# A weight load at the start of a TensorE-bound kernel is made to wait for a one-column activation

## The chip, the cores and the metric

The kernel runs on one core of one Trainium2 chip. The metric is device time in microseconds (us) of one execution. "Span" is the time from the first to the last instruction of a profiled execution; it is about 1.7 us shorter than the time of the same execution. The spread of executions is given as lowest to highest.

## The reference, cut to what matters

```
qkv = x @ wqkv                                  # x: 2048 x 1024, bf16
A:  pq, pk = phi(q), phi(k);  phi(t) = where(t > 0, t + 1, exp(t)) + 1e-6
    a = linear attention of pq, pk, v, 32 heads of 32, then @ wo
B:  sliding window of 8 keys, dilation 2, softmax, then @ wo   (own weights, same x)
out = g * a + (1 - g) * b,   g = sigmoid(sum(x * gate_w))
```

The kernel first computes K of branch A, which is x @ (1024 columns of wqkv), and for that it needs x transposed and these weights.

## The kernel before

The weights of K lie in two tiles, `WkA[0]` and `WkA[1]`: one for the first 512 columns ("first half"), one for the last 512 ("second half"). Each tile is loaded in four quarters of two 128-row blocks of the weights, 256 KB each. `xT` is x transposed by DMA. These are the loads at the start, in program order; SyncE (`nc.sync`) and ScalarE (`nc.scalar`) each issue on a DMA queue of their own:

```python
    nc.scalar.preload_act_table_set("natural_log_exp_and_others")
    ...
    def load_xT(k, t0, t1):
        nc.sync.dma_start_transpose(out=xT[:, 2 * k:2 * k + 2, t0 * P:t1 * P],
                                    in_=rows(x, t0 * P, t1 * P)[:, 2 * k * P:(2 * k + 2) * P])

    def load_wk(eng, k, h):
        eng.dma_start(out=WkA[h][:, 2 * k:2 * k + 2, :],
                      in_=A_wqkv[2 * k * P:(2 * k + 2) * P, D + 512 * h:D + 512 * h + 512]
                      .rearrange("(kt p) n -> p kt n", p=P))

    ones = nc.const_aps.tensor(1.0, [P, P], BF16)
    with tc.manual_schedule(engines={SP, mybir.EngineType.Activation}):
        load_wk(nc.scalar, 0, 0)                       # first half, first quarter
        first_act = consts.tile([P, 1], BF16, name="first_act")
        nc.scalar.activation(out=first_act[:], in_=ones[:, 0:1], func=ACT.Exp)
        load_wk(nc.scalar, 0, 1)                       # second half, first quarter
        load_xT(0, 0, 2)                               # first transpose
        load_xT(0, 2, 4)                               # second transpose
        for k in range(1, 4):
            load_wk(nc.sync, k, 0)
            load_xT(k, 0, 4)
            load_wk(nc.sync, k, 1)
        ...
```

TensorE runs 37 small warm-up matmuls and then the real ones. The order of its first sixteen is fixed: four with the first transpose and the first half, four with the second transpose and the first half, then eight with the second half.

```python
            warm_up(37)
            ...
            for k in range(4):
                for half in range(2):
                    for t in range(4):
                        for kt in (2 * k, 2 * k + 1):
                            project(first[4 * half + t], t, kt, half)
            ...
```

The softmax here doesn't subtract the row's maximum and nothing guards it: scores larger than these inputs give would overflow.

## Time and profile before

| | before |
|---|---|
| time, median of 3 (lowest to highest) | 474.03 us (473.62 to 474.06) |
| span of the profiled execution | 472.3 us |
| TensorE busy | 466.0 us |
| first real matmul | 5.56 us |

Two lines of the page: the busy time and share of each engine, and the chain of work that ended last, by engine.

```profile
PE 466.0 (99%) x5734; PEld 244.7 (52%) x5765; DVE 277.4 (59%) x601; ACT 169.1 (36%) x273; POOL 15.4 (3%) x30
...
PE 98%; DMA 1%; issue 0%; ACT 0%
```

TensorE is the limit nearly everywhere; the only other part of the chain is 1% of DMA. The chain in order of time says where that is (start, duration, what):

```profile
0.80 4.71 DMA xT<-in_A_x_dram
5.51 0.04 issue
5.56 3.16 PE pk_ps L169 x12
```

The first transpose holds the chain until it lands at 5.51 us. The timeline (start, duration, engine, line, operation, what it writes and reads; in brackets the idle time before it and what ended it), first for ScalarE and its DMA queue (ACTq), then for TensorE:

```profile
0.80 1.28 ACT L68 ACT_TABLE_LOAD   x1 [0.80 <-PEq L628]
0.83 0.96 ACTq L98 DMA_DIRECT2D WkA<-in_A_wqkv_dram  x2
2.09 0.20 ACT L106 ACTIVATE first_act<-const-bfloat16-1.0 128x1 bf16<-128x1 bf16 x1
...
0.84 4.11 PE L175 MATMUL warm<-const-bfloat16-1.0 128*128 128x128 bf16 x37 [0.84 <-PEq L628]
5.56 3.81 PE L169 MATMUL pk_ps<-WkA,xT 128*128 128x512 bf16 x14 [0.61 <-DMA xT<-in_A_x_dram]
```

Both weight quarters are issued one right after the other (x2, from 0.83 us) although an activation stands between them in the program: ScalarE's sequencer passes the activation on to the engine, which is busy with its table load, and goes on to the next DMA. TensorE then idles for 0.61 us.

Two stretches of the table by windows (start:end, length, busy time of PE, PEld, DVE, ACT and POOL, clock record, DMA share, GB/s):

```profile
3.50:4.00 0.50, 0.50 (x8) 0.50 (x6) 0.00 (x0) 0.00 (x0) 0.00 (x0) 1.00 1.14 288
4.00:4.50 0.50, 0.50 (x7) 0.50 (x6) 0.00 (x0) 0.00 (x0) 0.00 (x0) 1.00 1.08 331
```

The DMA engines are full here (shares of 1.14 and 1.08: by this measure no idle time is left). The clock column shows 1.00 also where the trace has no clock record yet, as here, so it does not show that the clock was full. By the trace's packets it is mostly the second weight quarter that moves in these two stretches.

### The profile page before, as it was taken

What the parts mean: (1) busy time and instruction counts of PE and PEld (TensorE: products, weight loads), DVE (VectorE), ACT (ScalarE), POOL (GpSimd) and SP (SyncE); (2) the same over time, 40 slices, a digit from 0 to 9 for tenths busy, and PEclk for the clock granted to TensorE, in tenths of its full rate; (3) what the DMA queues carried; (4) which work ended last, traced back from release to release, by engine and by line L of the source; (5) the groups of instructions that cost most, each with busy time, mean ns of one, the idle gap of its engine ahead of it and who ended that gap; (6) DMA issues with size and microseconds to landing.
All of it is one profiled execution on the core that took longest, in us unless ns stands there. A gap on an engine that the chain in (4) does not pass through costs nothing.

```text
span 472.3 us, 13144 instructions
## 1 busy us (share of the span) xinstructions
PE 466.0 (99%) x5734; PEld 244.7 (52%) x5765; DVE 277.4 (59%) x601; ACT 169.1 (36%) x273; POOL 15.4 (3%) x30
## 2 busy tenths in 40 slices
PE   8999999999999999999999999999999999999997
PEld 5444444445444444445666666666664444444444
DVE  0496689990329999999567676767560049800000
ACT  1343321102443333333555555555551134221122
POOL 3300000500000000000000000000000000000000
PEclk9999999999999999999999999999999999999999
DMA  8999970000634233527326526452563933211001
GB/s 212 212 242 374 348 239 0 0 1 0 203 123 125 95 141 129 156 96 247 107 54 108 105 53 95 100 95 51 92 158 79 196 97 78 71 53 46 34 33 46
DMA packets 98780, 55.40 MB, mean 117 GB/s; under 512 B 70178, under 2 KB 90658, under 8 KB 98722
## 3 DMA queue, kind: packets, MB, share of 16 engines
q1 hardware_dynamic: 93282, 49.84, 41.1%
q10 hardware_dynamic: 5440, 4.72, 3.0%
q8 instruction: 45, 0.74, 0.7%
q14 instruction: 13, 0.11, 0.1%
HBM read 26.10 MB, written 15.86 MB: 89 GB/s over the span
## 4 chain that ended last, share of the span: by engine, by line
PE 98%; DMA 1%; issue 0%; ACT 0%
PE q_ps L388 27%; PE d_ps L585 12%; PE pk_ps L169 12%; PE p_ps L295 12%; PE g_ps L220 12%; PE e_ps L585 11%; PE p_ps L331 9%; PE po L467 2%; PE s2b L445 2%; DMA xT<-in_A_x_dram 1%; PE kv_ps L240 0%; PE w_ps L283 0%; ACT osb L590 0%
## 5 line engine op out<-in xcount | busy, mean ns | idle before, releaser
L388 PE MATMUL q_ps<-xT,WqB 64*64 64x512 bf16 x1024 | 68.3, 377 | 0.0
L388 PE MATMUL q_ps<-xT,WkB 64*64 64x512 bf16 x1024 | 67.9, 377 | 0.0
L156 DVE TENSOR_SCALAR e<-e 128x512 f32<-128x512 f32 x64 | 27.0, 423 | 64.3 <-ACT e L155 64.3
L295 PE MATMUL p_ps<-WvB,xT 128*128 128x512 bf16 x250 | 57.3, 379 | 0.5 <-issue 0.3
L169 PE MATMUL pk_ps<-WkA,xT 128*128 128x512 bf16 x251 | 55.6, 381 | 0.9 <-DMA xT<-in_A_x_dram 0.6
L220 PE MATMUL g_ps<-pk,xrow 128*128 128x512 bf16 x251 | 55.2, 379 | 0.3
L450 ACT ACTIVATE PT<-s2b 128x928 bf16<-128x928 f32 (+4 forms) x40 | 34.2, 854 | 45.5 <-PE s2b L445 45.5
L452 DVE TENSOR_TENSOR PT<-PT,mask 128x928 bf16<-128x928 bf16 (+4 forms) x40 | 23.6, 590 | 38.2 <-ACT PT L450 38.2
L331 PE MATMUL p_ps<-WqA,xT 128*128 128x512 bf16 x187 | 43.1, 379 | 0.3
L585 PEld LDWEIGHTS <-pqT 128*128 128x128 bf16 x272 | 26.0, 98 | 29.8 <-issue 0.4
L585 PEld LDWEIGHTS <-OBT 128*128 128x128 bf16 x272 | 26.0, 98 | 29.3
L169 PEld LDWEIGHTS <-xT 128*128 128x128 bf16 x256 | 25.1, 98 | 31.2 <-DMA xT<-in_A_x_dram 0.9
L220 PEld LDWEIGHTS <-xrow 128*128 128x128 bf16 x256 | 25.0, 98 | 30.2
L295 PEld LDWEIGHTS <-xT 128*128 128x128 bf16 x256 | 24.6, 98 | 30.0 <-issue 0.9
L388 PEld LDWEIGHTS <-WkB 64*64 64x64 bf16 x1024 | 31.7, 107 | 15.4 <-issue 0.4
L388 PEld LDWEIGHTS <-WqB 64*64 64x64 bf16 x1024 | 31.4, 106 | 15.4 <-issue 0.7
L155 ACT ACTIVATE e<-pk_ps 128x512 f32<-128x512 f32 x32 | 18.9, 597 | 40.8 <-PE pk_ps L169 36.6
L300 ACT CAST tmp<-p_ps 128x512 bf16<-128x512 f32 x32 | 18.8, 590 | 37.9 <-PE p_ps L295 29.2
L585 PE MATMUL d_ps<-WoA,pqT 128*128 128x512 bf16 (+1 forms) x133 | 30.7, 369 | 0.2
L585 PE MATMUL d_ps<-WoB,OBT 128*128 128x512 bf16 (+1 forms) x134 | 30.7, 369 | 0.1
L331 PEld LDWEIGHTS <-xT 128*128 128x128 bf16 x192 | 18.8, 98 | 22.7
L585 PE MATMUL e_ps<-WoB,OBT 128*128 128x512 bf16 (+2 forms) x133 | 29.7, 363 | 0.2
(62 smaller groups left out, 484.6 us busy)
## 6 DMA issues: line engine op xcount, KB each, us to landing
vd<-tmp SPq DMA_DIRECT2D x16, 264.0 KB
xrow<-in_A_x_dram SPq DMA_DIRECT2D x4, 1024.0 KB
out_dram<-osb ACTq DMA_DIRECT2D x31, 128.0 KB
pqd<-tmp SPq DMA_DIRECT2D x12, 256.0 KB
WvA<-in_A_wqkv_dram SPq DMA_DIRECT2D x2, 1024.0 KB
WoA<-in_A_wo_dram SPq DMA_DIRECT2D x2, 1024.0 KB
WvB<-in_B_wqkv_dram SPq DMA_DIRECT2D x2, 1024.0 KB
WqA<-in_A_wqkv_dram SPq DMA_DIRECT2D x2, 1024.0 KB
```

Of the source, the lines that this page charges most:

```text
L155: nc.scalar.activation(out=e[:], in_=pj[:], func=ACT.Exp)
L156: nc.vector.tensor_scalar(out=e[:], in0=e[:], scalar1=1.0, scalar2=1e-6, op0=ALU.min, op1=ALU.add)
L169: nc.tensor.matmul(pj[:], lhsT=xT[:, kt, t * P:(t + 1) * P], rhs=WkA[half][:, kt, :], start=(kt == 0), stop=(kt == KT - 1))
L220: nc.tensor.matmul(pj[:], lhsT=xrow[:, t, kt * P:(kt + 1) * P], rhs=pk[:, t, half * 512:(half + 1) * 512], start=(t == 0), stop=(t == NB - 1))
L295: nc.tensor.matmul(st["pj"][:], lhsT=xT[:, kt, t * P:(t + 1) * P], rhs=WvB[half][:, kt, :], start=(kt == 0), stop=(kt == KT - 1))
L300: nc.scalar.copy(out=v[:, half * 16:(half + 1) * 16, 0:Dh], in_=st["pj"][:].rearrange("p (h e) -> p h e", h=16))
L331: nc.tensor.matmul(st["pj"][:], lhsT=xT[:, kt, t * P:(t + 1) * P], rhs=WqA[half][:, kt, :], start=(kt == 0), stop=(kt == KT - 1))
L388: nc.tensor.matmul(banks[o][64 * j:64 * j + 64, :], lhsT=lhsT(r, kt, j), rhs=rhs(r, kt), start=first and kt == 0, stop=kt == KT - 1, skip_ ...
L445: nc.tensor.matmul(s2b[64 * par:64 * par + 64, pair, :, o:o + w], lhsT=kts[c][r, par, k0:k0 + 64], rhs=qz[r, :, par, q0 % 512:q0 % 512 + w ...
L450: nc.scalar.activation(out=pt[:, :, 0:W_], in_=s2b[:].rearrange("p a b s -> p (a b) s")[:, :, 0:W_], func=ACT.Exp, scale=SCALE)
L452: nc.vector.tensor_tensor(out=pt[:, :, 0:W_], in0=pt[:, :, 0:W_], in1=mask[:, None, base:base + W_].broadcast_to([P, 4, W_]), op=ALU.mult)
L585: nc.tensor.matmul(st["ps"][:, 0:n], lhsT=lhsT, rhs=W[c0 // 512][:, c, c0 % 512:c0 % 512 + n], start=(side == 0 and c == 0), stop=(side == ...
```

## The change

The activation now writes a column of the second half's tile. The load of that quarter overwrites the column, so it has to wait for the activation. The result is the same. The intent: keep the quarter off the DMA engines while the first transpose, on which TensorE waits, is under way. The whole diff:

```diff
         load_wk(nc.scalar, 0, 0)
-        first_act = consts.tile([P, 1], BF16, name="first_act")
-        nc.scalar.activation(out=first_act[:], in_=ones[:, 0:1], func=ACT.Exp)
+        nc.scalar.activation(out=WkA[1][:, 0, 0:1], in_=ones[:, 0:1], func=ACT.Exp)
         load_wk(nc.scalar, 0, 1)
         load_xT(0, 0, 2)
         load_xT(0, 2, 4)
```

## The prediction

> **What bounds the kernel now.** TensorE. The page gives PE 466.0 of 472.3 us (99%); the chain that ended last is 98% PE, 1% DMA. The list of waits has three for PE: 0.8 us at launch, 0.61 us for the first DMA of xT, 0.3 us of issue. So a moved load can help only at the start. The timeline shows 37 warm-up matmuls from 0.84 to 4.95 us, then idle until the first real matmul at 5.56.
>
> **What the change does.** The 0.205 us activation now writes a column of the second half's weight tile, so the DMA that fills that quarter (256 KB, queued from ScalarE) must wait for it. Before, ScalarE's sequencer issued both weight quarters at 0.83 and 1.35 us (0.446 us each), while the 1.28 us table load and the activation (2.09 to 2.29) still ran; the order staggered nothing. The Trainium skill ("DMA: Bandwidth & Descriptors", Anatomy of one DMA) says that DMA engines don't wait on semaphores; the wait sits on the issuing sequencer. So I expect the second issue at about 2.3 to 2.4 us: about 1.0 us later.
>
> **What it is worth.** Packets of the trace: the first quarter moves from 1.75 to 3.3 us, the first xT transpose from 2.75 to 3.9, the second quarter from 3.5 to 4.5, though issued 1.7 us earlier: it queues behind the first quarter. The first transpose's last data packets end near 3.9, yet its closing 4-byte packets run from 4.25 on and it lands at 5.51. A later transpose has its closing packets right behind the data. So about 0.4 us of the first landing looks like contention with the second quarter (same skill page, Queues, rings and completion order: each engine alternates between queues at packet granularity). The delayed issue could give back at most the 0.61 us wait. But an issue at 2.35 to 2.8, plus the 0.5 us from end of issue to first packet seen for the first quarter, starts its packets at about 3.3 anyway, nearly where they start now. So I expect part: first real matmul at about 5.25 us, 0.3 us earlier, range 0 to 0.6.
>
> **What could be lost.** The second quarter lands now at 5.19 us; delayed by up to 1 us, at most about 6.2. PE needs it after eight matmuls (about 2.3 us in the present timeline), at 7.5 us or later. The second transpose (now 5.91) is needed four matmuls after the first; 6.3 would still just do. Later loads keep about 1 us of slack. Nothing after the start changes.
>
> **Prediction.** 474.03 - 0.3 = 473.7 us, 80% range 473.0 to 474.5. Faster by over 2%: 0.01; within 2%: 0.98; slower by over 2%: 0.01. A 2% move would need 9.5 us; the stretch touched is 5 us.
>
> **What the profile would show.** Right: the second weight issue on ScalarE's queue at about 2.3 us, after the activation; PE's wait on "DMA xT" below 0.61 us (0.1 to 0.5), first real matmul at 5.0 to 5.5 us; no new PE wait on WkA; PE busy still near 466. Wrong: the first xT landing unchanged (then contention was not its cause); a PE wait on WkA between 6 and 9 us.
>
> **What would make it wrong.** The second transpose, not the second quarter, may be what holds back the first one's completion: then nothing moves. The postponed packets may delay the second transpose and create a wait after four matmuls. Removing the one-column tile can shift later tiles' addresses, whose effect I can't cost.

## The result, and the profile after

| | before | after |
|---|---|---|
| time, median of 6 (lowest to highest) | 473.86 us (473.54 to 475.84) | 475.36 us (474.67 to 476.80) |
| ratio | | 1.0029, 95% interval 1.0006 to 1.0052 |
| span of the profiled execution | 472.3 us | 473.0 us |

A ratio is the mean time of one kernel's fast runs over that of the other's in the same rounds, so it is not quite the ratio of the medians. The change is within 2%, but it costs about 1.5 us in the median where 0.3 us of gain was expected. The range of 473.0 to 474.5 us was missed.

The same views of the kernel after: the chain in order of time, then the timeline of ScalarE and of TensorE.

```profile
2.16 5.23 DMA xT<-in_A_x_dram
7.39 0.05 issue
7.44 4.71 PE pk_ps L168 x21
```

```profile
0.82 0.45 ACTq L98 DMA_DIRECT2D WkA<-in_A_wqkv_dram  x1
2.09 0.21 ACT L105 ACTIVATE WkA<-const-bfloat16-1.0 128x1 bf16<-128x1 bf16 x1
2.32 0.41 ACTq L98 DMA_DIRECT2D WkA<-in_A_wqkv_dram  x1
...
0.84 4.11 PE L174 MATMUL warm<-const-bfloat16-1.0 128*128 128x128 bf16 x37 [0.84 <-PEq L627]
5.29 1.04 PE L168 MATMUL pk_ps<-WkA,xT 128*128 128x512 bf16 x4 [0.35 <-DMA xT<-in_A_x_dram]
7.44 1.90 PE L168 MATMUL pk_ps<-WkA,xT 128*128 128x512 bf16 x8 [1.11 <-DMA xT<-in_A_x_dram]
```

The second quarter is issued at 2.32 us, right after the activation ends at 2.30: the intended wait is there. The first real matmul starts at 5.29 us, 0.26 us earlier. But after four matmuls TensorE stands still until 7.44 us, and the chain names the load it waits for: issued at 2.16 us, it is the second transpose, and it lands at 7.39 us. Before, it had landed at 5.91 us and nobody waited for it.

The table by windows, same stretches:

```profile
3.50:4.00 0.50, 0.50 (x8) 0.50 (x7) 0.00 (x0) 0.00 (x0) 0.00 (x0) 1.00 0.28 61
4.00:4.50 0.50, 0.50 (x7) 0.50 (x6) 0.00 (x0) 0.00 (x0) 0.00 (x0) 1.00 0.51 95
```

Where 288 and 331 GB/s had flowed, 61 and 95 flow now. By the packets, the quarter moved from 3.4 to 4.6 us before; after, it trickles from 3.9 to 6.5 us, together with the second transpose (3.6 to 6.0 us).

How much of the time is decided in these first microseconds? Let the "fifth matmul" be the first real one that needs the second transpose. It starts at 6.83 us before and 7.44 after, 0.605 us later, and the spans differ by 0.7 us. The 0.605 us split into three parts, read from the starts of the single matmuls:

- the first matmul starts 0.263 us earlier (gain);
- the first two take 0.442 us instead of 0.829, because in the trace before they ran at half speed: the clock record of that trace begins at full speed at 6.41 us, that of the trace after at 4.83 us (0.387 us; nothing shows that this comes from the change: in e1 below, the same kernel as after, the record begins at 5.66 us);
- the third and fourth, with the wait, take 1.701 us instead of 0.446 (loss of 1.255 us).

### The profile page after: what moved, and what is told of

Its sections match the earlier page's. It is cut to its first block, busy times and chain, and to the rows that moved or that the text cites. A ratio compares the mean times of both kernels' runs of the same rounds, so it can differ in the third digit from the quotient of the medians.

```text
span 473.0 us, 13175 instructions
## 1 busy us (share of the span) xinstructions
PE 467.7 (99%) x5765; PEld 245.4 (52%) x5765; DVE 277.3 (59%) x601; ACT 169.2 (36%) x273; POOL 15.3 (3%) x30
## 3 DMA queue, kind: packets, MB, share of 16 engines
q10 hardware_dynamic: 5440, 4.72, 3.2%
## 4 chain that ended last, share of the span: by engine, by line
PE 98%; DMA 1%; SPq 0%; ACT 0%; issue 0%
PE q_ps L387 27%; PE d_ps L584 12%; PE p_ps L294 12%; PE g_ps L219 12%; PE pk_ps L168 12%; PE e_ps L584 12%; PE p_ps L330 9%; PE po L466 2%; PE s2b L444 2%; DMA xT<-in_A_x_dram 1%; PE kv_ps L239 0%; PE w_ps L282 0%; SPq L94 0%; ACT osb L589 0%
## 5 line engine op out<-in xcount | busy, mean ns | idle before, releaser
L584 PE MATMUL e_ps<-WoA,pqT 128*128 128x512 bf16 (+2 forms) x136 | 30.0, 364 | 0.0
```

What stands on the lines that cost most here:

```text
L584: nc.tensor.matmul(st["ps"][:, 0:n], lhsT=lhsT, rhs=W[c0 // 512][:, c, c0 % 512:c0 % 512 + n], start=(side == 0 and c == 0), stop=(side == ...
```

## The experiments

The theory after the result: *the postponed quarter meets the second transpose, delays its landing, and TensorE waits.* The rivals: shifted addresses (a tile was removed); chance, by the phase of the TensorE clock; any wait on that load costs time. All times in this table are read from each kernel's trace, in us from the start of the span. A landing is the last of the load's completion records. Runs e1 to e4 were made on one chip, e5 to e8 on a second, e9 to e11 on a third, each with the kernel before beside them (medians 473.62, 473.48 and 473.73 us); the ratios compare within a chip.

| kernel | quarter issued | first transpose lands | second transpose lands | quarter lands | first real matmul | fifth real matmul | full clock from | span |
|---|---|---|---|---|---|---|---|---|
| before | 1.35 | 5.51 | 5.91 | 5.19 | 5.56 | 6.83 | 6.41 | 472.3 |
| after | 2.32 | 5.25 | 7.39 | 7.16 | 5.29 | 7.44 | 4.83 | 473.0 |
| e1, after again | 2.32 | 4.10 | 6.52 | 6.22 | 4.74 | 6.56 | 5.66 | 472.0 |
| e2, addresses only | 1.34 | 5.35 | 5.56 | 5.01 | 5.40 | 6.27 | 5.10 | 471.7 |
| e3, wait for VectorE | 1.49 | 5.84 | 6.19 | 5.56 | 5.88 | 7.57 | 9.70 | 474.2 |
| e10, two activations more | 3.00 | 4.66 | 6.53 | 6.33 | 4.74 | 6.57 | 5.35 | 472.1 |
| e4, four activations more | 3.69 | 4.73 | 5.34 | 7.85 | 4.78 | 6.46 | 6.68 | 472.5 |
| e5, after with idle time filled | 2.33 | 5.95 | 8.01 | 7.78 | 5.99 | 8.28 | 4.42 | 474.0 |
| e6, before with idle time filled | 1.34 | 5.31 | 5.53 | 4.96 | 5.38 | 6.62 | 6.13 | 472.1 |
| e7, from SyncE's queue | 3.44 | 4.75 | 5.33 | 6.28 | 4.79 | 5.71 | 4.92 | 471.2 |
| e8, second load plain | 2.33 | 4.16 | 6.24 | 6.41 | 4.56 | 6.29 | 4.33 | 471.8 |
| e9, an eighth from ScalarE | 2.33 and 3.44 | 4.92 | 5.48 | 6.79 | 4.96 | 5.84 | 4.72 | 472.2 |
| e11, e7 in another order | 3.44 | 4.71 | 5.52 | 6.91 | 4.76 | 5.63 | 3.63 | 473.1 |

One question is answered by the table at once. Span minus the start of the fifth matmul is 465.5 to 465.8 us for before, after, e1, e2, e5, e6, e7, e8 and e10. For e3, e4, e9 and e11 it is larger (466.0 to 467.5), and in their traces more half-speed matmuls or later waits stand just behind the fifth matmul. So nothing after the start tells these kernels apart, and the time is to be explained in the first 12 us.

### e1: the kernel after, once more

No edit.

> The changed kernel unaltered, for a second trace and more runs on the chip that runs the others. Main theory (the postponed weight quarter travels together with the second xT transpose and delays it): second transpose lands at 7.2 to 7.6 us again, one PE wait of 1.0 to 1.3 us after the fourth real matmul, first real matmul near 5.3 us; 0.5 to 1.5 us slower than before. Rival (chance phase of the TensorE clock, which reached full speed at 6.4 us in the trace before and at 4.8 us in the trace after): the difference in time vanishes or changes sign with more runs, and the landing is not fixed.

Measured: 475.08 us (473.79 to 476.78, 6 runs), before 473.62 us (473.51 to 474.26, 11 runs), ratio 1.0032, interval 1.0016 to 1.0049. The loss is there again on another set of runs, so the chance of one comparison is not its cause. The landing of 6.52 us and the single wait of 0.3 us by the waits view missed the expected numbers: they belong to the profiled execution, which with 473.79 us was the fastest of the six. How late the second transpose lands differs between executions of the same kernel.

```profile
2.16 4.36 DMA xT<-in_A_x_dram
6.52 0.05 issue
6.56 1.90 PE pk_ps L168 x8
```

In the chain the load issued at 2.16 us still stands last before the matmuls go on: the same wait, shorter.

### e2: the addresses alone

```diff
-        first_act = consts.tile([P, 1], BF16, name="first_act")
-        nc.scalar.activation(out=first_act[:], in_=ones[:, 0:1], func=ACT.Exp)
+        gw_row = consts.tile([P, D], BF16, name="gw_row")     # moved up from below
+        nc.scalar.activation(out=gw_row[:, 0:1], in_=ones[:, 0:1], func=ACT.Exp)
```

> The one-column tile is removed as in the change, so later tiles lie at the same addresses as after, but the activation writes a column of another tile that is loaded much later; the second weight quarter does not wait. Main theory: like before, second issue on ScalarE's queue at 1.35 us, second transpose lands near 5.9 us, no PE wait after the fourth matmul, time within 0.3 us of before. Rival (shifted addresses cost the time): like after, 0.5 to 1.5 us slower.

Measured: 473.64 us (473.35 to 474.53), ratio 1.0001, interval 0.9989 to 1.0013. The second transpose landed at 5.56 us and there was no second wait: sixteen matmuls in a row.

```profile
5.40 3.84 PE L168 MATMUL pk_ps<-WkA,xT 128*128 128x512 bf16 x16 [0.45 <-DMA xT<-in_A_x_dram]
```

The removed tile costs nothing; that rival falls.

### e3: an earlier wait, on another engine

```diff
+        nc.vector.memset(WkA[1][:, 0:2, :], 0.0)
         load_wk(nc.scalar, 0, 0)
```

> The kernel before, plus a VectorE memset over the second half's first weight quarter, so that its load waits for VectorE instead of ScalarE and is issued earlier than after: at about 1.4 to 1.8 us, ahead of the second transpose's issue at 2.16 us. Main theory, in the form that the quarter must be queued ahead of the second transpose: second transpose lands by 6.1 us and no second PE wait; time within 0.5 us of before. Rival (any semaphore wait on that load costs time): a second PE wait of about 1 us.

Measured: 474.00 us (473.52 to 475.99), ratio 1.0016, interval 1.0000 to 1.0031. The load waited for VectorE and was issued at 1.49 us. The second transpose landed at 6.19 us, just over the expected 6.1, and TensorE had no second wait. So in this trace a wait on that load does the transpose no harm by itself; it put the issue off by only 0.15 us. The times alone do not decide it: the interval reaches 1.0031, as much as the loss of the kernel after, and two of the six executions took 475.61 and 475.99 us. The profiled one is the longest, at 475.99 us. TensorE's timeline shows two things, the idle time before the first real matmul and the length of the next eight:

```profile
5.88 3.60 PE L170 MATMUL pk_ps<-WkA,xT 128*128 128x512 bf16 x8 [0.94 <-DMA xT<-in_A_x_dram]
```

Eight matmuls in 3.60 us is 0.43 us from start to start instead of 0.216: half speed, and the clock record begins at full speed only at 9.70 us. Whether the late start of the matmuls brought this on is not shown: e5 below starts them later still, at 5.99 us, with the clock full from 4.42 us.

### e4 and e10: a later wait

Both add activations of 128 columns into the quarter, after the one of the change; four in e4, two in e10.

```diff
         nc.scalar.activation(out=WkA[1][:, 0, 0:1], in_=ones[:, 0:1], func=ACT.Exp)
+        for _ in range(4):                                    # e10: range(2)
+            nc.scalar.activation(out=WkA[1][:, 0, 0:P], in_=ones, func=ACT.Exp)
         load_wk(nc.scalar, 0, 1)
```

> The kernel after, plus four activations over 128 columns of the same quarter, so that its load is issued only at about 3.5 us, after the second transpose has been issued (2.16 to 3.40 us). If the loss comes from the overlap of the two issues: second transpose lands near 5.3 us, first matmul near 5.2 us, no wait for the transpose; the quarter lands at about 6.5 us, before it is needed at about 7.0; 0.3 to 0.7 us faster than before. If any weight packets that travel with the transpose slow it: it still lands after 6.3 us and PE waits 0.3 us or more after the fourth matmul.

Measured for e4: 474.43 us (474.04 to 475.10), ratio 1.0017, interval 1.0004 to 1.0030. Issued at 3.69 us, after the second transpose's issue had ended, the quarter left the transposes alone: they landed at 4.73 and 5.34 us. That part of the theory held. The gain did not come: the quarter itself landed at 7.85 us, not 6.5, and TensorE waited for it after eight matmuls, as the bracket of the second line shows:

```profile
4.78 2.82 PE L170 MATMUL pk_ps<-WkA,xT 128*128 128x512 bf16 x8
7.89 1.47 PE L170 MATMUL pk_ps<-WkA,xT 128*128 128x512 bf16 x5 [0.29 <-DMA WkA<-in_A_wqkv_dram]
```

> The kernel after with two added activations of 128 columns: the second weight quarter is issued at about 3.0 us, still while SyncE issues the second transpose (2.16 to 3.40), but its packets should begin when most of the transpose's have gone. If overlap of the two issues is enough for the loss: second transpose lands after 6.3 us. If the packets must be in flight together: it lands before 6.0 us, between the 5.3 us of the run that issued at 3.7 us and the 6.5 to 8.0 us of those at 2.3 us.

Measured for e10: 473.75 us (473.53 to 473.99), before 473.73, ratio 0.9998, interval 0.9984 to 1.0011. The second transpose landed at 6.53 us. By the words of the expectation this speaks for the overlap of the two issues, but the packets show something between: all but two of the transpose's data packets had started by 4.75 us, the weight quarter's ran mostly from 4.5 to 5.9 us, and the transpose's 32 small closing packets started only from 5.25 us on. So here the data got through and the closing came late, while the weights moved. Overlap of the issues alone is not established as the cause. TensorE waited after its fourth matmul here too, but the fifth started no later than in the trace before (6.83 us), since the first had come at 4.74 us:

```profile
4.74 1.33 PE L170 MATMUL pk_ps<-WkA,xT 128*128 128x512 bf16 x4
6.57 2.76 PE L170 MATMUL pk_ps<-WkA,xT 128*128 128x512 bf16 x12 [0.51 <-DMA xT<-in_A_x_dram]
```

### e5 and e6: the idle time filled with matmuls

Both use 43 instead of 37 warm-up matmuls. e5, made from the kernel after, has twelve more small matmuls between the fourth and the fifth:

```diff
+                            if (k, half, t, kt) == (0, 0, 2, 0):
+                                for _ in range(12):
+                                    nc.tensor.matmul(first[7][:, 0:P], lhsT=ones, rhs=ones, start=True, stop=True)
                             project(first[4 * half + t], t, kt, half)
```

> The kernel after with the idle time of TensorE in the start filled: 43 warm-up matmuls instead of 37, and 12 more small matmuls after the fourth real matmul, into a bank that is overwritten later. The loads are those of after. Theory A (the wait for the second transpose costs mainly by letting the TensorE clock stay at or fall back to half speed for one more 3.4 us period, as the spread of after from 473.8 to 476.8 us suggests): the slow runs vanish, all runs within 1.2 us of each other, median 0.7 us or more below after's 475.1. Theory B (it costs only its own length, the clock is chance): median and spread like after's, or up to 0.3 us slower because of the added matmuls.

> The kernel before with 43 instead of 37 warm-up matmuls, so that TensorE idles at most 0.1 us before the first real matmul. Theory A: the clock reaches full speed no later than about 7.7 us in any run, no run over 474.5 us; median within 0.4 us of before, since half-speed matmuls up to 6.4 us cost the trace before only 0.4 us. Theory B: nothing changes, or up to 0.3 us slower.

Measured for e5: 475.48 us (475.00 to 475.92), ratio 1.0035, interval 1.0019 to 1.0051. All six within 0.9 us, as theory A had it, but the median did not fall by 0.7 us; it stayed. Measured for e6: 473.81 us (473.51 to 474.44), ratio 1.0002, interval 0.9987 to 1.0017: nothing, as both theories allowed. So the clock is not the main cost of the change. In e5's trace the clock was full from 4.42 us on, before the first real matmul, and the loss was there all the same, through the landing of the second transpose at 8.01 us:

```profile
5.99 1.04 PE L168 MATMUL pk_ps<-WkA,xT 128*128 128x512 bf16 x4 [0.88 <-DMA xT<-in_A_x_dram]
6.87 0.87 PE L190 MATMUL pk_ps<-const-bfloat16-1.0 128*128 128x128 bf16 x12
8.28 1.03 PE L168 MATMUL pk_ps<-WkA,xT 128*128 128x512 bf16 x4 [0.55 <-DMA xT<-in_A_x_dram]
```

Two of the twelve executions of the kernel after took 476.8 us, with a mean granted clock of 0.996. The mean counts only the time from the first clock record on (e3's late first record left its mean at 1.000). Half speed for 3.4 us of 475 would give 0.996; 3.4 us is the step between the lengths of the full-speed records in these traces (464.213 us in e3, 471.039 in e5 and e11, 467.626 in all others). No trace of such an execution exists, so that these two lost a stretch of clock is likely, not shown.

### e7 and e11: the quarter on SyncE's queue

```diff
-        load_wk(nc.scalar, 0, 1)
         load_xT(0, 0, 2)
         load_xT(0, 2, 4)
+        load_wk(nc.sync, 0, 1)
         for k in range(1, 4):
-            load_wk(nc.sync, k, 0)                            # these two lines: e11 only
             load_xT(k, 0, 4)
+            load_wk(nc.sync, k, 0)
```

> The kernel before, with the second weight quarter issued from SyncE's queue behind both transposes instead of from ScalarE's. If two queues in flight together slow the transposes: both transposes run undisturbed, first real matmul at 4.7 to 5.0 us, second transpose lands at about 5.3 us, the quarter (issued at 3.44) lands at about 6.3, no PE wait for either; later loads about 0.6 us later, the third transpose at about 8.4, just in time; 0.3 to 0.8 us faster than before. If the transposes are slow for another reason: first matmul at 5.3 us or later and no gain.

Measured for e7: 473.59 us (472.90 to 473.75), before 473.48, ratio 0.9994, interval 0.9979 to 1.0009. With nothing on the other queue beside them, the transposes landed at 4.75 and 5.33 us and the matmuls ran without a wait from 4.79 us:

```profile
4.79 4.53 PE L169 MATMUL pk_ps<-WkA,xT 128*128 128x512 bf16 x19
```

This execution has the shortest span of all, 471.2 us, but it is one of six; the other five took 473.58 to 473.75, no less than before. In the trace the third transpose, of the next step, landed at 8.19 us and was needed at about 8.25 (the weight load that uses it started at 8.23, its matmul at 8.30, without a gap). If it lands a little later in the others, the gain is gone. e11 tested this.

> The variant that issued the second weight quarter from SyncE's queue behind both transposes, and in its second step of the loop also the transpose ahead of the weights. That variant's third transpose landed at 8.19 us and was needed at 8.25 us. If this just-in-time landing is why its first matmul at 4.8 us gave nothing in most runs: third transpose lands at 7.6 us or earlier, time 0.4 to 0.8 us below before in the median. If chance of the clock is why, the median stays within 0.2 us of before.

Measured for e11: 474.57 us (473.79 to 474.88), before 473.73, ratio 1.0012, interval 1.0000 to 1.0025. Both forecasts missed. The third transpose came earlier, at 7.91 us, but the weights that had changed places with it landed at 10.22 us instead of 7.24, and TensorE waited for them. The chain:

```profile
5.36 4.86 DMA WkA<-in_A_wqkv_dram
10.22 0.04 issue
10.26 1.89 PE pk_ps L169 x8
```

So in this trace the two loads have no slack: the one that was moved back came late. What held the other five executions of e7 back stays open, since there are no traces of them.

### e8: is it the transpose?

```diff
-        load_xT(0, 2, 4)
+        nc.sync.dma_start(out=xT[:, 0:2, 2 * P:4 * P],
+                          in_=A_wqkv[0:2 * P, 0:2 * P].rearrange("(kt p) n -> p kt n", p=P))
```

> The kernel after with the second transpose replaced by a plain load of as many bytes into the same place (the result is wrong on purpose). If what is slow in after is a transpose sharing the engines with a plain load: the plain second load lands by 5.9 us in spite of the weight quarter beside it, no PE wait after the fourth matmul. If any two loads of the two queues slow each other as much: it lands after 6.3 us as in after.

Measured: wrong result, so its time (473.50 us, 2 runs) says little. The plain load of the same bytes landed at 6.24 us, between the two expectations, and TensorE waited 0.70 us for it after the fourth matmul:

```profile
4.56 1.02 PE L169 MATMUL pk_ps<-WkA,xT 128*128 128x512 bf16 x4
6.29 2.98 PE L169 MATMUL pk_ps<-WkA,xT 128*128 128x512 bf16 x12 [0.70 <-DMA xT<-in_A_wqkv_dram]
```

So a transpose isn't needed for the wait; a plain load beside the postponed quarter makes TensorE wait as well. One thing else changed: SyncE issued the plain load in 0.56 us instead of 1.24, so the weights behind it were issued at 2.77 us instead of 3.44 and may have had a part in the delay. How early the plain load lands with nothing beside it was not measured.

### e9: fewer bytes on the other queue

```diff
-        load_wk(nc.scalar, 0, 1)
+        load_part(nc.scalar, 0, 16)       # 16 of 128 partitions, 32 KB
         load_xT(0, 0, 2)
         load_xT(0, 2, 4)
+        load_part(nc.sync, 16, P)         # the other 224 KB
```

> The kernel after, but only an eighth of the second weight quarter (16 of 128 partitions, 32 KB) is issued from ScalarE's queue at about 2.3 us; the other seven eighths go from SyncE's queue behind the second transpose. If the number of weight bytes that share the engines with the second transpose is what delays it: it lands by 5.8 us, no PE wait after the fourth matmul. If a start of any load on the other queue while the transpose is being issued is enough: it still lands after 6.3 us and PE waits 0.4 us or more.

Measured: 473.84 us (473.38 to 473.94), before 473.73, ratio 0.9996, interval 0.9981 to 1.0012. Issued at 2.33 us as in the kernel after, the small piece did the second transpose no harm: it landed at 5.48 us and TensorE ran on.

```profile
4.96 3.85 PE L172 MATMUL pk_ps<-WkA,xT 128*128 128x512 bf16 x16
```

This is the clearest of the eleven: same wait, same moment of issue, an eighth of the bytes, and the delay is gone, and with it the loss (the interval ends at 1.0012; that of e1, the kernel after, begins at 1.0016). So the wait, and an issue at that moment, do not delay the transpose by themselves; it takes the bulk of the quarter beside it. Whether it is the moving of its packets or their preparation that delays the transpose, this does not separate. (Later loads come late instead: TensorE stops for 0.23 us after the eighth real matmul and for 0.61 us after the sixteenth, and the time ends where before is.)

## Why the prediction was wrong

- *The second issue moves to 2.3 to 2.4 us, behind the activation.* Right: 2.32 us.
- *The first landing comes earlier, the first real matmul at about 5.25 us.* Right in the trace after (5.29 us); earlier still in e1 (4.74). There the load landed at 4.10 us, but the last warm-up matmul had started at 4.63, so nothing more could be gained. e4, e7, e9, e10 and e11, with no full quarter beside the first transpose, had it land at 4.66 to 4.92 us; before, e2, e3 and e6, with the quarter early, at 5.31 to 5.84 us. So the reading that the early quarter cost the first landing some tenths of a microsecond fits these. But e5 had 5.95 us with the late issue, so it does not hold in every execution.
- *The quarter's packets would start at about 3.3 us anyway.* Too early: 3.94 us in after, 3.76 in e5, 3.44 in e1, which is 0.7 to 1.2 us from the end of the issue where the estimate took 0.5 from the very first load. The larger miss is how long they ran: 2.2 to 3.3 us, to 6.50, 7.10 and 5.62 us; before, 1.1 us, to 4.55.
- *"The second transpose (now 5.91) is needed four matmuls after the first; 6.3 would still just do."* This is the step that failed. It allowed the second transpose a delay of 0.4 us without a wait, so the sum has no loss for it; the traces show landings at 7.39, 6.52 and 8.01 us (after, e1, e5), 0.6 to 2.1 us later, and TensorE waiting for them in each (1.11 us in after). The prediction did name this wait as what might go wrong, but gave it no weight in the sum.
- *A gain of 0.3 us in the sum.* In its place: 0.26 us earlier at the first matmul and 1.255 us lost at the fifth in the trace after. That trace is of the fastest of its six executions (474.67 us), and e1's of the fastest of its six. e5's, with the landing at 8.01 us, is of an execution at 475.76 us, near the median of the kernel after. So the 1.5 us of the medians fit landings near 8 us; a trace of a median execution of the unaltered kernel after was not taken.
- *Nothing after the start changes; within 2%.* Right: the span from the fifth matmul on is 465.5 us before and after.

The intent overlooked that the early quarter used time in which the DMA engines had little else to do. In e4, where the quarter is issued late enough to leave the transposes alone, the engines move 120 GB/s from 3.5 to 4.5 us; before, 309. Sent early, the quarter fills that hole. Postponed, it trickles beside the second transpose, and the weights behind them, of the next step, land at 7.85 us instead of 6.69.

What stays open: why the DMA engines are so poorly used from 3.5 to 4.5 us in all nine traces in which the quarter was not issued by 1.5 us (78 to 147 GB/s; where it was, 302 to 328). Two loads beginning together is not needed for it: e4 (120) and e7 (125), where the quarter moves later, lie between after (78) and e1 (147). Open too is why the landing differs by 1.5 us between executions. The Trainium skill ("DMA: Bandwidth & Descriptors", Queues, rings and completion order) says that an engine alternates between queues by packets. The trace agrees so far as packets of both queues start in the same quarter of a microsecond, but sharing alone would not leave the engines idle.

## What to carry to other kernels

Before you hold a load back in favour of another, look in the table by windows whether the DMA engines have anything else to move at that time, and list for every load behind it when it lands and when it is needed. Here a load postponed by 1 us met the next urgent one, which landed 0.6 to 2.1 us later, and the kernel lost 1.5 us in the median. With one engine busy for 99% of the span, the start decided nearly all differences between these kernels, and the number to compare is the start of the first instruction after the last start-up wait, in several executions, since one trace can be the luckiest.

## What the Trainium skill lacked or had wrong

None of these points contradicts its page; they are gaps.

- "DMA: Bandwidth & Descriptors", Issuing engines are not separate DMA queues: it says that issuing from several engines at once saves only the sequencers' time. It does not speak of the moment of the issue, and that made the difference here: 302 to 328 GB/s from 3.5 to 4.5 us in the four traces in which ScalarE's queue got its second load at 1.3 to 1.5 us, 78 to 147 in the nine in which the load came later or on the other queue.
- The same page has no figure for the slow beginning of a load beside another: in the trace after, the quarter's packets from 4.0 to 4.75 us took 110 to 130 ns each on average (over half of them 46 ns, the others 76 to 389), those in the middle of the first quarter 46 ns.
- "DMA: Bandwidth & Descriptors", Anatomy of one DMA — SWDGE (gpsimd) path, says that the wait of a DMA sits on the issuing sequencer, in a section on GpSimd's path; that it is so for a load from ScalarE too is shown here (activation ends at 2.30 us, issue starts at 2.32).
- "TensorE: Matmul & The Clock Gate", Why this matters for your kernels, warns of idle gaps over about 3 us and gives no figure for shorter ones during the warm-up. In e3 the clock reached full speed only at 9.70 us, with 0.94 us idle before the first real matmul; in before, with 0.61 us idle, at 6.41 us. That the shorter gap was the cause is not tested. The page's free-running window of about 3.4 us (Part 1) fits the spread of 3.63 to 6.68 us in the other traces and the 3.413 us by which the lengths of the full-speed records differ, and its half speed is seen: 0.427 us from start to start against 0.216.
